# A retention and mixture-of-experts kernel on one core: first loads swapped, two weight blocks ahead of the sorted rows, count sums on GpSimd, totals and head rows one step earlier

## The chip, the cores and the metric

The kernel runs on one core of a Trainium2 chip. The core has a matrix engine (TensorE, PE in the profile; its weight loads are a row of their own, PEld), a vector engine (VectorE, DVE), an activation engine (ScalarE, ACT), a general engine (GpSimd, POOL) and an engine that here mostly issues transfers (SyncE, SP; its rows in the profile are SPq). Each takes its own instructions in order and waits for others by semaphores. Transfers between device memory and on-chip memory (SBUF) run on 16 DMA engines. Matmuls write to PSUM, which has eight banks of 2 KB in each of the 128 partitions. The metric is the device time of one execution in microseconds (us).

## What is computed

Four sequences of 768 tokens with 8 heads of 64 go through retention (attention without softmax, whose state decays by a factor for each head), and the 3072 resulting rows of 512 through a layer of 8 experts. Each row goes to the expert with the largest gate logit alone.

```python
def _attn_ref(q, k, v):                      # B=4, H=8, S=768, D=64
    gamma = 1.0 - 2.0 ** (-5.0 - np.arange(H))
    for t in range(S):
        state = gamma[None, :, None, None] * state + np.einsum('bhd,bhe->bhde', k[:, :, t], v[:, :, t])
        y[:, :, t] = scale * np.einsum('bhd,bhde->bhe', q[:, :, t], state)

def _moe_ref(x, w_gate, w_output_gate, w1, w2):   # x 3072x512, w1 8x512x1024, w2 8x1024x512
    logits = x @ w_gate
    e_idx = np.argmax(logits, axis=1)
    gate_w = softmax(logits)[np.arange(N), e_idx]
    eom = 1.0 / (1.0 + np.exp(-(x @ w_output_gate)))
    for e in range(E):
        mask = e_idx == e
        h = np.maximum(x[mask] @ w1[e], 0.0)
        out[mask] = gate_w[mask, None] * eom[mask, e, None] * (h @ w2[e])
```

## The kernel before

The instructions of each engine stand in the order in which the program is written; no scheduler moves them. So an instruction that waits holds everything that is written behind it for the same engine.

**Start.** SP loads the keys of chunk 0, then the queries (one load serves two chunks of a channel), then those of chunk 1. PE runs matmuls on zeros (`warm_up`) until the keys have come; `kt_block` turns the keys and `qt_block` the queries with PE transposes.

**Chunk loop.** 24 chunks of 128 tokens, one a step, in two channels: even steps belong to channel 0, odd ones to channel 1. A step `n` multiplies the queries with the carried state (`inter`, L348) and with the keys (`scores`, L356, into the banks `s`), masks the scores on DVE (`masked`, L364, `am`), multiplies with the values (`values`, L374, into the banks `y`), scales on DVE (`outputs`, L394, `yt`) and updates the state (`state`, L383, copied to `sd` on ACT). GpSimd scales the values of the next chunk (`prep_v`, L310, `vs`).

Two chunks form a group for the routing, which runs through the following steps. At the end of an odd step PE makes the group's logits (L403, into the bank `misc`), and ACT keeps them (`lt`, L408). In the next even step PE turns them (`turn_logits`, L414), eight small DVE operations choose the expert (`route1`, one-hot `oh`) and ACT takes the exponentials (`exps`). In the odd step after that PE counts the rows ahead of each row (`counts`, L450 to L455), DVE adds the one-hots to the running sums (`acc`, L460) and works out the row's place (`rk` L462, `pos` L465), all in `route2`, ahead of `values` in the program; and at the end of the step, behind the next group's logits, four DVE operations make the gate weight (`gates`, L473 to L477, with scratch in `misc`). PE transposes the finished chunk (`tokens`, L486, into one of two PSUM buffers `px`), ACT scales it by the gate (`rows_out`, L493, `row`), and GpSimd scatters the rows to their expert's region of a sorted table `srt` in device memory (`scatter`, L502).

In step 14 and again in step 18 PE adds up the running sums (`totals`, L517, in `misc`, right after `inter`): the first chooses the early expert, whose number SP loads one step later, the second (with `cj` on DVE, L657) its count so far. From step 17 on weight blocks come in: a block is 128 of an expert's 1024 inner columns, 512 KB in three transfers (`load_weights`, L171 and L175, into four buffers `raw`). ACT rounds it to `whi` (`split_high`, L187, L188), DVE and GpSimd subtract to `wlo` (`split_low`, L195, L196), so that a product is made of three matmuls. After step 20 SP loads the first 256 sorted rows of the early expert (`head_load`, L537); `head_prep` turns them on DVE, half in step 22 and half at the end of step 23, where the row numbers are worked out too (`token_ids`).

**After the loop.** The head (first 256 rows of the early expert, L564 and L582) keeps PE busy in pieces (`run_head`), while the last group is routed and scattered, the experts are ordered by their counts (`order`) and GpSimd clears the row behind each region (`clear`). Then SP loads the sorted rows of pass 0, the other 192 columns of the early expert (`load_x(0)`, L815, `xl`), and seven register loads of `order` (L953). Pass 0 and the seven experts run over 8 blocks each: `mm1` (L873, into `h`), `relu1` (ACT `hh` L882, DVE `hl` L883), `mm2` of the block before (L896, into `a`). Weight blocks are loaded in order, each once its buffer is free; pass 0 starts with blocks 8 and 9, then the next expert's rows are loaded (`load_x(1)`), then block 10 and on. In the last four blocks of a pass `prep_x` turns a quarter of the next expert's rows each (DVE `xt` L836, ACT `xh` L837, DVE `xw` L838); GpSimd sends the finished rows out (`emit`, L203). The last expert's blocks are accumulated row by row (`stage2_last`, L924) and sent by `emit_last`.

Of the kernel before, what the change touches and what calls it, by code (L numbers as in the profile page):

```python
# [33 lines left out]
def retention_moe_kernel(  # L34
# [191 lines left out]
    with ExitStack() as actx:  # L226
# [57 lines left out]
        for b in range(2):  # L284
            nc.vector.memset(sp[b], 0.0)
        load_k(0)
        load_q(0, 0)
# [168 lines left out]

        def route2(grp):
            n = len(grp)
            oh = rt.pop("oh")
            nc.vector.tensor_tensor(out=acc[:, 0:n], in0=acc[:, 0:n], in1=oh, op=ALU.add)  # L460
# [8 lines left out]
        def gates(grp):  # L469
            n = len(grp)  # L470
            ex = rt.pop("ex")
            se, den = small[:, 10 * E:10 * E + 2], small[:, 10 * E + 2:10 * E + 4]
# [71 lines left out]
        def head_prep(g):  # L544
# [7 lines left out]
            if g == 1:  # L552
                hd["idx"] = hpool.tile([P, HEAD // 32], I32, name="idx0")
                tmp = hpool.tile([P, HEAD // 32], I32, name="tmp0")
                token_ids(hd["idx"], t[:, :, P], slot[:, 0:HEAD // 32], cnt0, tmp, False)

        def head_stage1(f):
# [3 lines left out]
            for r, ls in (("xh", (hi, lo)), ("xl", (hi,))):  # L561
                for dc in range(NDC):
# [59 lines left out]
        warm_up(misc, 9)  # L622
        kt_block(0)
        warm_up(misc, 2)
        for r in range(2):
            q_copy(0, 0, r, nc.vector)
        for r in range(2):
            qt_block(0, 0, r, nc.vector if r == 1 else None)
# [10 lines left out]
        for n in range(NCH):  # L639
# [10 lines left out]
            if n in w_at:  # L650
                load_weights(w_at[n])
            inter(n)
            if n == PICK_AT:
                by = rank_key(totals(n), io8)
            if n == EARLY_AT:
                cj = sm.tile([P, E], F32, name="cj", tag="cj")
                nc.vector.scalar_tensor_tensor(out=cj, in0=totals(n), scalar=1.0, in1=first, op0=ALU.mult, op1=ALU.mult,  # L657
                                               accum_out=cnt0)
# [18 lines left out]
            if even and n >= 4:  # L677
                tokens(n - 3)
# [16 lines left out]
            if even and n >= 4:  # L695
                rows_out(n - 3)
            values(n)
            outputs(n)
            state(n)

            for t in turn.get(n, ()) if not soon else ():
                qt_block(*t)
            if not even and n >= 3:
                tokens(n - 3)
            if not even:
# [4 lines left out]
                if grp:  # L710
                    gates(grp)
# [11 lines left out]
            if n - 1 in w_at:  # L723
                split_high(w_at[n - 1])
# [8 lines left out]
            if n == LOAD_AT:  # L733
                head_load()
# [15 lines left out]
        counts(grp, True)  # L750
        route2(grp)
        gates(grp)
# [47 lines left out]
    with ExitStack() as mctx:  # L800
# [149 lines left out]
        arms = {}  # L950
        load_x(0)
        for r in range(1, E):
            rank_e[r] = nc.values_load(order[0:1, r - 1:r], engines=(ET.SP,), min_val=0, max_val=E - 1)  # L953
# [15 lines left out]
        loaded = split = NF  # L969
        for s in range(NS + 1):  # L970
# [168 lines left out]
```

## Time and profile before

| | us |
|---|---|
| median of 3 runs (lowest to highest) | 444.88 (443.98 to 445.35) |
| profiled execution | 442.21 |
| its span in the profile | 440.4 |
| PE busy (share of the span) | 417.7 (95%) |
| VectorE busy | 230.8 (52%) |
| ScalarE busy | 191.2 (43%) |
| GpSimd busy | 255.8 (58%) |
| mean granted TensorE clock | 0.996 |

The profile is of one execution; its own time is 442.21 us, and the span leaves out what lies around the instructions. Busy shares are averages over stages that have different limits. PE's stages are the start (to about 14 us), the chunk loop (to 138), the head (to 164), pass 0 (to 191), the seven other experts (to 428) and the tail. Times in the rows are counted from the start of the span.

### The profile page before, as it was taken

To read this page: it belongs to the slowest core of one execution; us is meant where nothing else is said; L and a number is where in the kernel's file an instruction comes from. 1 tells how busy PE (TensorE), PEld (TensorE's weight loads), DVE (VectorE), ACT (ScalarE), POOL (GpSimd) and SP (SyncE) were. 2 spreads that over 40 slices of the span, in tenths; PEclk is the share of its full clock that TensorE was granted. 3 is DMA by queue.
4 is the path that set the end of the run, shared out by engine and by line. 5 is a ranking of instruction groups with operands and counts; after the bars stand their busy time and mean duration, and the time that the engine had idled before them with its cause. 6 is when DMAs were issued, how large, how long until landed. Compare 5 with 4: busy or idle time off the path is not lost.

```text
span 440.4 us, 10495 instructions
## 1 busy us (share of the span) xinstructions
PE 417.7 (95%) x3600; PEld 382.8 (87%) x3600; DVE 230.8 (52%) x593; ACT 191.2 (43%) x375; POOL 255.8 (58%) x292
## 2 busy tenths in 40 slices
PE   8999899999997999899999999998999999999992
PEld 4778687787786999789999999998999999999881
DVE  3465767666678854672553544454355356354110
ACT  2456455555656423553443443443354354353110
POOL 1555644444549605577237687685776877884712
PEclk9999999999999999999999999999999999999998
DMA  9999989679446529999368459549458848740102
GB/s 200 194 225 267 245 211 230 161 191 245 128 132 208 199 77 229 229 207 235 100 164 205 125 174 227 167 147 215 148 154 186 219 153 190 224 125 10 50 16 71
DMA packets 128381, 75.75 MB, mean 172 GB/s; under 512 B 57748, under 2 KB 116504, under 8 KB 128288
## 3 DMA queue, kind: packets, MB, share of 16 engines
q1 hardware_dynamic: 120896, 59.15, 56.5%
q0 software_dynamic: 5776, 14.76, 9.5%
q8 instruction: 61, 1.00, 1.0%
q10 hardware_dynamic: 1616, 0.57, 0.7%
q14 instruction: 32, 0.26, 0.2%
HBM read 59.71 MB, written 15.30 MB: 170 GB/s over the span
## 4 chain that ended last, share of the span: by engine, by line
PE 78%; DVE 6%; DMA 4%; issue 4%; ACT 3%; POOL 1%; SPq 1%; DVEq 0%; POOLq 0%; ACTq 0%
PE h L873 25%; PE a L896 24%; PE s L356 5%; PE y L374 5%; PE y L348 2%; PE px L486 2%; PE y L564 2%; PE pq L329 2%; DMA qn<-in_q_dram 2%; PE pk L315 2%; PE a L924 2%; PE s L582 2%; PE st L383 2%; PE misc L403 2%; DMA xl<-srt 1%
## 5 line engine op out<-in xcount | busy, mean ns | idle before, releaser
L196 POOL TENSOR_TENSOR wlo<-raw,whi 128x512 fp32r<-128x512 f32 x59 | 78.3, 1328 | 56.0 <-ACT whi L188 46.0
L203 POOL DMA_INDIRECT out_dram<-ot,idi x85 | 86.0, 1012 | 22.5 <-issue 17.7
L873 PE MATMUL h<-xh,whi 128*128 128x192 f32 (+7 forms) x256 | 85.1, 333 | 2.2 <-issue 1.5
L873 PE MATMUL h<-xw,whi 128*128 128x192 f32 (+7 forms) x256 | 85.0, 332 | 0.2 <-DVE xw L838 0.2
L873 PE MATMUL h<-xh,wlo 128*128 128x192 f32 (+7 forms) x256 | 84.7, 331 | 0.0
L883 DVE SCALAR_TENSOR_TENSOR hl<-h,hh 128x192 fp32r<-128x192 f32 (+7 forms) x64 | 35.5, 555 | 88.5 <-ACT hh L882 88.4
L896 PE MATMUL a<-hh,whi 128*128 128x192 f32 (+6 forms) x224 | 74.6, 333 | 1.5 <-ACT hh L882 1.5
L896 PE MATMUL a<-hl,whi 128*128 128x192 f32 (+6 forms) x224 | 74.6, 333 | 0.1
L896 PE MATMUL a<-hh,wlo 128*128 128x192 f32 (+6 forms) x224 | 74.3, 332 | 0.0
L882 ACT ACTIVATE hh<-h 128x192 fp32r<-128x192 f32 (+7 forms) x64 | 31.3, 489 | 77.4 <-PE h L873 77.4
L195 DVE TENSOR_TENSOR wlo<-raw,whi 128x512 fp32r<-128x512 f32 x62 | 42.7, 689 | 31.5 <-ACT whi L187 29.1
L187 ACT CAST whi<-raw 128x512 fp32r<-128x512 f32 x64 | 39.5, 617 | 41.0 <-PE a L896 34.4
L873 PEld LDWEIGHTS h<-xh,whi 128*128 128x128 f32 x256 | 48.2, 188 | 3.5 <-issue 1.8
L873 PEld LDWEIGHTS h<-xw,whi 128*128 128x128 f32 x256 | 48.2, 188 | 1.0 <-DVE xw L838 0.5
L873 PEld LDWEIGHTS h<-xh,wlo 128*128 128x128 f32 x256 | 48.2, 188 | 0.2
L502 POOL DMA_INDIRECT srt<-row,pos x24 | 24.6, 1026 | 36.0 <-ACT qr L321 22.3
L896 PEld LDWEIGHTS a<-hh,whi 128*128 128x128 f32 x224 | 42.2, 188 | 2.2 <-ACT hh L882 1.9
L896 PEld LDWEIGHTS a<-hl,whi 128*128 128x128 f32 x224 | 42.2, 188 | 0.7 <-DVE hl L883 0.4
L896 PEld LDWEIGHTS a<-hh,wlo 128*128 128x128 f32 x224 | 42.2, 189 | 0.3
L310 POOL TENSOR_TENSOR vs<-vn,gv 128x512 f32<-128x512 f32 x24 | 24.9, 1039 | 28.9 <-DMA vn<-in_v_dram 14.6
L188 ACT CAST whi<-raw 128x512 fp32r<-128x512 f32 x64 | 39.5, 616 | 0.4 <-DMA raw<-in_moe_w_dram 0.4
L364 DVE TENSOR_TENSOR am<-s,mask 128x512 f32<-128x512 f32 x48 | 30.9, 686 | 15.8 <-PE s L356 15.4
(170 smaller groups left out, 652.0 us busy)
## 6 DMA issues: line engine op xcount, KB each, us to landing
raw<-in_moe_w_dram SPq DMA_DIRECT2D x128, 128.0 KB, 4.1
raw<-in_moe_w_dram SPq DMA_DIRECT2D x64, 256.0 KB, 3.9
kn<-in_k_dram SPq DMA_DIRECT2D x24, 256.0 KB, 4.9
qn<-in_q_dram SPq DMA_DIRECT2D x12, 512.0 KB, 6.3
vn<-in_v_dram SPq DMA_DIRECT2D x23, 256.0 KB, 5.3
xl<-srt SPq DMA_DIRECT2D x12, 209.6 KB, 6.2
xl<-srt SPq DMA_DIRECT2D x8, 225.8 KB, 7.7
xl<-srt SPq DMA_DIRECT2D x8, 193.5 KB, 5.6
```

What stands on the lines that cost most here:

```text
L187: nc.scalar.copy(hi[:, 0], raw[:, 0])
L188: nc.scalar.copy(perm(hi), r2)
L195: (first or nc.vector).tensor_sub(lo[:, 0], raw[:, 0], hi[:, 0].bitcast(F32))
L196: (second or nc.gpsimd).tensor_sub(perm(lo), r2, perm(hi).bitcast(F32))
L203: st = nc.gpsimd.indirect_dma_start(out=dst, out_offset=bass.IndirectOffsetOnAxis(ap=idx, axis=0), in_=src, in_offset=None, bounds_check=n ...
L310: nc.gpsimd.tensor_mul(vs[i], vn.pop(i), gv[:, c, :].unsqueeze(2).broadcast_to([P, H, D]))
L364: nc.vector.tensor_tensor(out=a.rearrange("p s o t -> p (s o) t"), in0=sp[b].rearrange("p (x t) -> p x t", t=P), in1=mask.unsqueeze(1).bro ...
L502: s_ = nc.gpsimd.indirect_dma_start(out=srt, out_offset=bass.IndirectOffsetOnAxis(ap=rt.pop(("pos", i)), axis=0), in_=row.rearrange("p a x ...
L873: nc.tensor.matmul(ps[:, 0:C], l[:, 0, w], r[:, dc, 0:C], start=(n == 0), stop=(n == 3 * NDC - 1))
L882: nc.scalar.activation(hh, ps[:, 0:C], AF.Relu)
L883: nc.vector.scalar_tensor_tensor(out=hl, in0=ps[:, 0:C], scalar=0.0, in1=hh.bitcast(F32), op0=ALU.max, op1=ALU.subtract)
L896: nc.tensor.matmul(accs[d][:, 0:C], l[:, 1, w], r[:, 0:C], start=(f == 0 and n == 0), stop=(f == NF - 1 and n == 2))
```

## The change

It has these parts.

1. Start: the queries of chunk 0 are loaded ahead of its keys, and copied and turned ahead of them; the copies are spread over DVE and ACT, and two of the matmuls on zeros go.
2. The running sums (`acc`) are added on GpSimd (`add_counts`), for all groups but the last.
3. `gates` moves from the end of the odd step to right behind `route2`; its scratch is a corner of the bank `s` instead of `misc`.
4. `totals` with what reads it moves from step 14 to the end of step 13, and from step 18 to the end of step 17.
5. Some transposes (`tokens`) of the odd steps go ahead of the values, and those of steps 22 and after the loop are moved; `split_high` goes ahead of the values in even steps.
6. `head_load` stands at the start of step 20, `head_prep(0)` at the end of step 21, and the row numbers (`head_ids`) behind the loop. `head_stage1` multiplies the first half of the columns with all three parts, then the second.
7. Behind the head's routing SP loads one register, weight blocks 8 and 9, then pass 0's rows, then the six other registers. In pass 0 the next expert's rows and block 10 therefore come first.
8. Tail: the last block but one is accumulated for two row groups before the last block begins.

```diff
-        load_k(0)
         load_q(0, 0)
+        load_k(0)
...
+        def add_counts(grp, eng):
+            eng.tensor_tensor(out=acc[:, 0:len(grp)], in0=acc[:, 0:len(grp)], in1=rt["oh"], op=ALU.add)
+
         def route2(grp):
             n = len(grp)
             oh = rt.pop("oh")
-            nc.vector.tensor_tensor(out=acc[:, 0:n], in0=acc[:, 0:n], in1=oh, op=ALU.add)
...
-        def gates(grp):
+        def gates(grp, tmp):
+            ex = rt.pop("ex")
             n = len(grp)
-            ex = rt.pop("ex")
-            se, den = small[:, 10 * E:10 * E + 2], small[:, 10 * E + 2:10 * E + 4]
+            se, den = tmp[:, 0:2], tmp[:, 2:4]
...
-            for r, ls in (("xh", (hi, lo)), ("xl", (hi,))):
-                for dc in range(NDC):
+            for r, ls, dcs in [(r, ls, g) for g in ((0, 1), (2, 3)) for r, ls in (("xh", (hi, lo)), ("xl", (hi,)))]:
+                for dc in dcs:
...
+        for r in range(2):
+            q_copy(0, 0, r, nc.vector if r == 0 else nc.scalar)
+        for r in range(2):
+            qt_block(0, 0, r, nc.vector)
         kt_block(0)
-        warm_up(misc, 2)
-        for r in range(2):
-            q_copy(0, 0, r, nc.vector)
-        for r in range(2):
-            qt_block(0, 0, r, nc.vector if r == 1 else None)
...
+            if n == LOAD_AT:
+                head_load()
             inter(n)
-            if n == PICK_AT:
-                by = rank_key(totals(n), io8)
-            if n == EARLY_AT:
-                cj = sm.tile([P, E], F32, name="cj", tag="cj")
...
                 counts(grp)
+                add_counts(grp, nc.gpsimd)
                 route2(grp)
+                gates(grp, sp[0][:, 0:4])
...
+            fill = not even and n > 4 and not turn.get(n, ())
...
+            if fill:
+                tokens(n - 3)
...
-            if n == LOAD_AT + 2:
-                head_prep(0)
-            if even and n >= 4:
+            if even and 4 <= n < NCH - 2:
                 rows_out(n - 3)
+            if even and n - 1 in w_at:
+                split_high(w_at[n - 1])
             values(n)
             outputs(n)
             state(n)
+            if n == NCH - 2:
+                tokens(n - 3)
+                rows_out(n - 3)
...
+            if n == PICK_AT - 1:
+                by = rank_key(totals(n), io8)
+            if n == EARLY_AT - 1:
+                cj = sm.tile([P, E], F32, name="cj", tag="cj")
...
-            if not even and n >= 3:
+            if not even and n >= 3 and not fill:
                 tokens(n - 3)
...
-                if grp:
-                    gates(grp)
...
-            if n == LOAD_AT:
-                head_load()
+            if n == LOAD_AT + 1:
+                head_prep(0)
...
         scatter(NCH - 4)
+        tokens(NCH - 3)
         turn_logits(grp)
-        tokens(NCH - 3)
+        split_high(NF - 4)
         rows_out(NCH - 3)
         route1(grp)
         exps(grp)
+        head_ids()
...
+        load_rank(1)
+        for s in (NF, NF + 1):
+            load_weights(s)
         load_x(0)
-        for r in range(1, E):
-            rank_e[r] = nc.values_load(order[0:1, r - 1:r], engines=(ET.SP,), min_val=0, max_val=E - 1)
+        for r in range(2, E):
+            load_rank(r)
...
-        loaded = split = NF
+        loaded, split = NF + 2, NF
...
-                for tb in range(NTB):
-                    for z in (NS - 2, NS - 1):
-                        stage2_last(z, tb)
+                for tb in range(2):
+                    stage2_last(NS - 2, tb)
+                for tb in range(NTB):
+                    if tb >= 2:
+                        stage2_last(NS - 2, tb)
+                    stage2_last(NS - 1, tb)
                     emit_last(tb)
```

What stands in a row on VectorE in an odd step of the loop, from the masks to the next step's masks, before (names are out<-in; `misc` and `s_126` are PSUM banks):

```order
L364 TENSOR_TENSOR am_448<-s_127,mask 128x512
L460 TENSOR_TENSOR acc<-acc,oh 128x16
L462 TENSOR_TENSOR misc<-misc,oh 128x16
L465 TENSOR_REDUCE pos<-misc 128x2
L394 TENSOR_TENSOR yt<-y_129,gq 128x2x128
L394 TENSOR_TENSOR yt<-y_130,gq 128x2x128
L473 TENSOR_REDUCE misc<-ex 128x2
L474 TENSOR_SCALAR misc<-misc 128x2
L475 SCALAR_TENSOR_TENSOR misc<-ex,misc 128x2
L477 RECIPROCAL gate<-misc 128x2
```

The same step on VectorE after the change:

```order
L364 TENSOR_TENSOR am_446<-s_127,mask 128x512
L464 TENSOR_TENSOR misc<-misc,oh 128x16
L467 TENSOR_REDUCE pos<-misc 128x2
L475 TENSOR_REDUCE s_126<-ex 128x2
L476 TENSOR_SCALAR s_126<-s_126 128x2
L477 SCALAR_TENSOR_TENSOR s_126<-ex,s_126 128x2
L479 RECIPROCAL gate<-s_126 128x2
L394 TENSOR_TENSOR yt<-y_129,gq 128x2x128
L394 TENSOR_TENSOR yt<-y_130,gq 128x2x128
```

The sum is gone from VectorE, and the four gate operations stand ahead of the two `yt`.

On PE the totals of step 13 and 14 (`ones_b` is a matrix of ones; after `state`, ahead of the transposes `px` and the logits, where the two lines of the difference stand with +):

```order
 L383 MATMUL st<-vs,kn 64x64 x8
-L486 MATMUL px<-ident,yt 128x128 x4
+L519 LDWEIGHTS ones_b
+L519 MATMUL misc<-acc,ones_b 128x8
+L519 LDWEIGHTS ones_b
+L519 MATMUL misc<-acc,ones_b 128x8
+L488 MATMUL px<-ident,yt 128x128 x4
 L403 MATMUL misc<-yt,wg 32x256 x4
 L348 MATMUL y_129<-qt,sd 64x128
```

They stood between the next step's state product (L348) and its scores (L356) before.

On SP, from pass 0's rows on, before (the two numbers behind a region are rows of 32 and their count):

```order
L815 DMA xl<-srt 32x6x129
L953 TENSOR_LOAD order
L953 ISA x2
L171 ISA
L171 DMA raw<-in_moe_w_dram 64x4x128
L175 ISA
L175 DMA raw<-in_moe_w_dram 128x512
L815 ISA
L815 DMA xl<-srt 32x14x129
```

The same place on SP after the change:

```order
L967 TENSOR_LOAD order
L967 ISA x2
L171 ISA
L171 DMA raw<-in_moe_w_dram 64x4x128
L175 ISA
L175 DMA raw<-in_moe_w_dram 128x512
L829 ISA
L829 DMA xl<-srt 32x6x129
L829 ISA
L829 DMA xl<-srt 32x14x129
```

Only one row of each repetition is shown. The two weight blocks stood between the two loads of sorted rows and now stand ahead of both.

## Rows read from the trace of the kernel before

**Rows 1.** Busy time of the engines: busy us (share of the span) xinstructions

```profile
PE 417.7 (95%) x3600; PEld 382.8 (87%) x3600; DVE 230.8 (52%) x593; ACT 191.2 (43%) x375; POOL 255.8 (58%) x292
```

**Rows 2.** What PE waited for, 10 to 140 us: us in total, times, longest

```profile
PE misc L414 <- DVE gate L477: 1.8, 2, 1.5
...
PE misc L517 <- DVE gate L477: 1.4, 2, 0.7
...
PE pq L329 <- ACT qr L321: 0.6, 1, 0.6
```

**Rows 3.** What PE waited for, 140 to 441 us

```profile
PE a L896 <- ACT hh L882: 1.5, 2, 0.8
```

**Rows 4.** Busy time by stage: length, engines (xinstructions), PE clock, DMA share, GB/s

```profile
138.00:164.00 26.00, 24.72 (x209) 24.51 (x210) 18.38 (x72) 11.45 (x26) 11.16 (x14) 1.00 0.48 157
164.00:191.00 27.00, 24.50 (x198) 23.05 (x197) 16.32 (x36) 12.54 (x27) 15.60 (x14) 1.00 0.93 224
```

**Rows 5.** The chain that ended last: start us, us, what

```profile
3.04 8.80 DMA qn<-in_q_dram
...
168.14 6.22 DMA xl<-srt
174.49 4.56 DMA raw<-in_moe_w_dram
```

**Rows 6.** Timeline of step 7: start us, us, engine line [idle before <-releaser]

```profile
49.52 2.83 DVE L460 TENSOR_TENSOR acc<-acc,oh 128x16 bf16<-128x16 bf16 x1
...
50.88 0.66 PE L486 MATMUL px<-ident,yt 128*128 128x128 f32 x4
...
51.28 1.03 POOL L310 TENSOR_TENSOR vs<-vn,gv 128x512 f32<-128x512 f32 x1
...
53.03 0.96 PE L403 MATMUL misc<-yt,wg 128*32 128x256 f32 x8 [1.49 <-DVE yt L394]
```

**Rows 7.** Timeline of step 19, VectorE and GpSimd

```profile
115.37 0.17 DVE L462 TENSOR_TENSOR misc<-misc,oh 128x16 f32<-128x16 f32 x1
115.38 1.26 POOL L196 TENSOR_TENSOR wlo<-raw,whi 128x512 fp32r<-128x512 f32 x1
```

**Rows 8.** Timeline of step 17, VectorE and PE

```profile
104.27 0.86 DVE L394 TENSOR_TENSOR yt<-y,gq 128x256 f32<-128x256 f32 x2
...
105.64 0.64 PE L403 MATMUL misc<-yt,wg 128*32 128x256 f32 x8
...
106.75 0.18 DVE L473 TENSOR_REDUCE misc<-ex 128x2 f32<-128x16 f32 x1 [1.62 <-ACT lt L408]
...
107.37 0.17 DVE L477 RECIPROCAL gate<-misc 128x2 f32<-128x2 f32 x1
```

**Rows 9.** Timeline of SP's queue in pass 0

```profile
162.15 1.46 SPq L171 DMA_DIRECT2D raw<-in_moe_w_dram  x2
...
167.05 1.94 SPq L815 DMA_DIRECT2D xl<-srt  x4
```

**Rows 10.** Timeline of pass 0, ScalarE, VectorE and PE

```profile
170.04 0.33 ACT L882 ACTIVATE hh<-h 128x192 fp32r<-128x192 f32 x1 [0.31 <-PE h L873]
...
172.72 0.33 ACT L882 ACTIVATE hh<-h 128x192 fp32r<-128x192 f32 x1 [0.31 <-PE h L873]
...
178.40 0.32 ACT L882 ACTIVATE hh<-h 128x192 fp32r<-128x192 f32 x1
...
180.22 0.64 DVE L836 STREAM_TRANSPOSE xt<-xl 128x448 f32<-128x448 f32 x1
...
190.61 0.47 PE L873 MATMUL h<-xw,whi 128*128 128x432 f32 x1 [0.19 <-DVE xw L838]
```

**Rows 11.** What SP's queue waited for, 140 to 200 us

```profile
SPq L815 <- DMA srt<-zrow,endr: 9.1, 1, 9.1
```

**Rows 12.** The first sorted rows `xl`, 150 to 170 us: uses (start us) and landing

```profile
L221 DVE TENSOR_TENSOR tmp<-tmp,xl x1: 170/170/170, 160.0 to 160.0; 128x6 int32<-128x6 int32 x1
...
DMA to landing us min/median/max: 2.1/2.1/2.1
```

More of the change, by code (lines that the diff above doesn't have):

```diff
@@ L285, in retention_moe_kernel @@
             nc.vector.memset(sp[b], 0.0)
+        load_q(0, 0)
         load_k(0)
-        load_q(0, 0)
         nc.scalar.activation(warm, warm, AF.Exp)
@@ L551, in head_prep, with head_ids @@
             nc.gpsimd.tensor_sub(hd["xl"][:, 2 * g:2 * g + 2], tp, hd["xh"][:, 2 * g:2 * g + 2].bitcast(F32))
[L552 to L555, printed above, removed]
+        def head_ids():
+            t = hd["t"]
+            hd["idx"] = hpool.tile([P, HEAD // 32], I32, name="idx0")
+            tmp = hpool.tile([P, HEAD // 32], I32, name="tmp0")
+            token_ids(hd["idx"], t[:, :, P], slot[:, 0:HEAD // 32], cnt0, tmp, False)
         def head_stage1(f):
@@ L651, in retention_moe_kernel @@
                 load_weights(w_at[n])
+            if n == LOAD_AT:
+                head_load()
             inter(n)
-            if n == PICK_AT:
-                by = rank_key(totals(n), io8)
-            if n == EARLY_AT:
-                cj = sm.tile([P, E], F32, name="cj", tag="cj")
-                nc.vector.scalar_tensor_tensor(out=cj, in0=totals(n), scalar=1.0, in1=first, op0=ALU.mult, op1=ALU.mult,
-                                               accum_out=cnt0)
             scores(n)
@@ L686, in retention_moe_kernel @@
                 counts(grp)
+                add_counts(grp, nc.gpsimd)
                 route2(grp)
+                gates(grp, sp[0][:, 0:4])
             soon = not even and len(turn.get(n, ())) == 1
+            fill = not even and n > 4 and not turn.get(n, ())
             if soon:
                 qt_block(*turn[n][0])
+            if fill:
+                tokens(n - 3)
             if even and n - 2 in w_at and n < 22:
                 split_low(w_at[n - 2])
-            if n == LOAD_AT + 2:
-                head_prep(0)
-            if even and n >= 4:
+            if even and 4 <= n < NCH - 2:
                 rows_out(n - 3)
+            if even and n - 1 in w_at:
+                split_high(w_at[n - 1])
             values(n)
@@ L699, in retention_moe_kernel @@
             state(n)
+            if n == NCH - 2:
+                tokens(n - 3)
+                rows_out(n - 3)
             for t in turn.get(n, ()) if not soon else ():
                 qt_block(*t)
-            if not even and n >= 3:
+            if n == PICK_AT - 1:
+                by = rank_key(totals(n), io8)
+            if n == EARLY_AT - 1:
+                cj = sm.tile([P, E], F32, name="cj", tag="cj")
+                nc.vector.scalar_tensor_tensor(out=cj, in0=totals(n), scalar=1.0, in1=first, op0=ALU.mult, op1=ALU.mult,
+                                               accum_out=cnt0)
+            if not even and n >= 3 and not fill:
                 tokens(n - 3)
@@ L722, in retention_moe_kernel @@
                 exps(grp)
-            if n - 1 in w_at:
+            if not even and n - 1 in w_at and n < NCH - 1:
                 split_high(w_at[n - 1])
@@ L750, in retention_moe_kernel @@
         counts(grp, True)
+        add_counts(grp, nc.vector)
         route2(grp)
-        gates(grp)
+        gates(grp, small[:, 10 * E:10 * E + 4])
         run_head(6)
@@ L950, in retention_moe_kernel, with load_rank @@
         arms = {}
+        def load_rank(r):
+            rank_e[r] = nc.values_load(order[0:1, r - 1:r], engines=(ET.SP,), min_val=0, max_val=E - 1)
+        load_rank(1)
+        for s in (NF, NF + 1):
+            load_weights(s)
         load_x(0)
-        for r in range(1, E):
-            rank_e[r] = nc.values_load(order[0:1, r - 1:r], engines=(ET.SP,), min_val=0, max_val=E - 1)
+        for r in range(2, E):
+            load_rank(r)
         PASS += [(rank_e[r] * REG, CAPS[r - 1]) for r in range(1, E)]
```

## The prediction

> **What bounds the kernel now.** I read the busy shares first: TensorE (PE) has work for 417.7 us of the span of 440.4 [rows 1], so some 22 us at most can be won without taking matmuls away, and this change takes almost none away. Next the waits of PE, in two stretches: in the chunk loop it stands still for single reasons of 0.6 to 1.5 us each [rows 2], after the loop for ScalarE's relu in the first pass of the sorted rows [rows 3]. The busy time by stage shows where the second kind lies: between 164 and 191 us PE works 24.50 of 27.00 us while the DMA engines are at 0.93, and in the stage before, 138 to 164, they are at 0.48 [rows 4]. Last the chain that ended last: it holds the landing of chunk 1's queries at the start, and much later the load of the second expert's rows followed by one weight block [rows 5]. So two sorts of edit can pay: one that takes a stall of PE out of the loop, and one that moves DMA work from 164 to 191 into the emptier stage ahead. The profiled execution took 442.21 us, 2.67 under the median of 444.88; the sum below is a difference against the profiled one and is taken off the median.
>
> **Queries ahead of keys: 0.** Chunk 1 is released by its queries, issued at 3.04 and landed 8.80 us later [rows 5]. The change only swaps the first two loads ahead of them, so the bytes in front stay the same. Chunk 0 may finish earlier and then waits for chunk 1. Bounds: 0.6 either way, what a late query copy cost PE in another step [rows 2].
>
> **Count sums on GpSimd: +1.8.** In step 7 the sum L460 on VectorE (DVE) took 2.83 us, 49.52 to 52.35, and ended when GpSimd's `vs`, begun at 51.28, ended after its 1.03. Behind it stood rank, position and the two `yt`, and PE, done with the transposes at 50.88 + 0.66 = 51.54, started the logits at 53.03 and took 0.96 for them [rows 6]; undisturbed logits take 0.64 [rows 8]. Without the sum, six small operations at 0.2 each (rank, position, four gates) let `yt` start about 50.8, and the logits run 51.54 to 52.18 and not to 53.99: 1.81. The lower end is 0, if the hold passes to the next DVE operation. Against that speaks step 19, where the rank L462 took 0.17 beside a GpSimd subtraction of 1.26 [rows 7]; I take the upper end. On GpSimd the small sum stands behind the scatter, and only the counts two steps later read it.
> The Trainium skill (GPSIMD Engine Reference, Key points) says that GpSimd shares its SBUF interfaces with VectorE and that VectorE instructions with two SBUF inputs contend. L460 has two such inputs, the rank reads one of its two from PSUM: by that rule the hold would not pass on and the time would be the 438.1 below; if any DVE operation can be held, it is the 439.9 of the fourth rival. Step 19 agrees with the rule, in one instance.
>
> **Totals one step up: +1.4.** The two totals waited 1.4 us in all, 0.7 the longer, for the gates that stood ahead of them in the same PSUM bank [rows 2]. Now they stand at the end of the odd step ahead of the transposes, and the gates write another bank. Their own matmuls stay. Bounds 0.8 to 1.45: the operation that reads the totals is one more of 0.2 on DVE, twice, and may push what comes next.
>
> **Gates in line: -0.15.** In step 17 the four gate operations ran from 106.75 to 107.37 + 0.17, 0.79 us, after the logits; DVE had idled 1.62 us before them, waiting for ScalarE to read the bank [rows 8]. Now they stand ahead of `yt`, in place of the sum. `yt` then starts some 0.6 us later than its 104.27, so it ends at about 105.75 and not at 105.13; the logits, at 105.64, need its second half only 0.32 later [rows 8]. So a usual step pays 0. In the last two odd steps the transposes move away from in front of the logits, there is less cover, and I charge 0.15. Worst end: 1.0 for those two and a few others; best 0.
>
> **Weight split ahead of the values: +0.4.** In step 19 PE waited 0.6 us for a query copy on ScalarE [rows 2] that was queued behind a weight cast. In steps 18, 20 and 22 the cast now goes earlier; bounds 0 to 0.6.
>
> **Loop end: +0.15.** The last turned logits waited 1.5 us for the gates [rows 2]. That wait goes, and transposes fill part of the place. But the head's second matmuls then wait for DVE, which still has the eight routing operations, the row numbers and a weight subtraction ahead of the half that they need, so most of the 1.5 comes back there. Bounds -0.5 to +0.6.
>
> **Two weight blocks ahead of the sorted rows: +3.4.** This is the large term. Before, two blocks held SP's queue from 162.15 until the second expert's rows went out at 167.05 [rows 9]. Those rows took 6.22 to land, and one block after them held the chain 4.56 more [rows 5]. ScalarE's relus stand at 170.04, 172.72 (2.68 apart, PE's pace) and then 178.40 [rows 10]. The two blocks now go out before the first sorted rows, while SP stood still for 9.1 us [rows 11] and the DMA engines were half idle [rows 4]. So the second expert's rows go out at 162.15 or a little before, 4.9 earlier, and the block behind them too. The late relu then falls at 172.72 + 2.68 = 175.40, 3.0 earlier. Behind it DVE prepares four pieces of the next expert's rows from 180.22 on; the last of these released PE at 190.61 [rows 10]. That train, 10.39 long, keeps its length, and starts 3.4 earlier: 3.0 from the relu, and 0.4 of the 1.82 between relu and first piece, where DVE reads row numbers. Bounds: 2.5 if a later block still lands late; 3.9 if half of the 1.82 goes.
>
> **What that does to the first sorted rows: -0.2.** Their load waited 9.1 us for the clearing of row ends [rows 11], landed in 2.1, and DVE used it at 160.0, at once [rows 12]. One MB of weights now moves while the clears do. The stage has room: half of its 26 us at 224 GB/s, the rate of the stage after [rows 4], is 2.9 MB. So I charge 0.2; the upper end is the first rival.
>
> **Tail: 0.** The two last weight blocks are accumulated in another order, with the same matmuls and the same three sends after them, which hide what PE gains. Bounds 0 to 0.8, the price of a wait for a relu in the first pass [rows 3].
>
> **Sum.** 1.8 + 1.4 - 0.15 + 0.4 + 0.15 + 3.4 - 0.2 = 6.8, so 442.21 becomes 435.4 profiled, and the median 444.88 becomes **438.1**.
>
> **Rivals.**
> First: the weight blocks make the first sorted rows late. For it: SP issues both, and the blocks now stand ahead; the second expert's rows took 6.22 in a full stage [rows 5], the first ones 2.1 [rows 12], 4.1 less. Against it: the half-idle stage. If all 4.1 fell on PE, 6.8 + 0.2 - 4.1 = 2.9 are left: 442.0.
> The Trainium skill (DMA: Bandwidth & Descriptors, Queues, rings and completion order) states that each DMA engine takes the descriptors of one ring in order, so that what SP issued first is fetched first; this speaks for the rival, and no row of before shows the two transfers in that order.
> Second: pass 0 keeps its length because the DMA engines stay at 0.93 there [rows 4] and later blocks arrive as late as before. Then 3.4 falls away: 441.5.
> Third, **slower**: the gates are not covered. They are 0.79 us in each of 11 odd steps; if DVE's work ahead of `yt` set each step's end, that is 8.7, against gains of 6.95 without this term: 1.75 slower, 446.6. It decides from 6.95 / 11 = 0.63 us per step. Against it: the cover in step 17 [rows 8], and the place that the sum leaves.
> Fourth: the hold of step 7 passes to another DVE operation, or returns in another step: 439.9.
> Fifth: nothing of it moves the end, since each stall is replaced by the next one: 444.9.
>
> **How the numbers follow.** Chances: forecast, with its small terms, 0.60; late first rows 0.08; pass 0 as long 0.12; hold moved 0.11; no change 0.05; slower 0.04. All upper ends together win 9.75 (0.6 + 1.8 + 1.45 + 0 + 0.6 + 0.6 + 3.9 + 0 + 0.8): 435.1. Low ends of the forecast (0.8 for the totals, 2.5 for the pass, 0 for the split) give 440.2; the second rival, which the range must also hold, 441.5. So the range is 435.1 to 441.6. About 0.3% (1.3 us) is what a measurement of this kernel can tell from no change. Faster 0.90, same 0.06, slower 0.04.
>
> **What would show it.** Right: no sum on DVE in the loop, and the logits of step 7 right behind the transposes; no wait for a gate in PE's list; the second expert's rows issued about 5 us earlier against the head's end; the relus of pass 0 evenly 2.7 apart; the last prepared piece no longer 18 us behind the relu at 172.72 but under 15. Wrong: DVE's first use of the sorted rows over 1 us later against the head's end, `yt` ending well after the transposes in most odd steps, or weight waits in pass 0 as before.

## The result, and the profile after

The changed kernel takes 437.66 us (437.14 to 438.06, 4 runs) against 444.43 (443.12 to 445.35, 4 runs) beside it: ratio 0.9849, 95% interval 0.982 to 0.9878, that is 6.8 us, between 5.4 and 8.0. The forecast was 438.1, 6.8 less than 444.88. The profiled execution took 437.51 us with a span of 435.7; the profiled one of before took 442.21, which is below every one of before's four runs here. So the two profiles differ by only 4.7, and a good part of this text is about the other 2.

The busy times after answer [rows 1]: PE is as busy as before, in a shorter span.

```profile
PE 417.4 (96%) x3598; PEld 381.7 (88%) x3598; DVE 224.9 (52%) x582; ACT 189.7 (44%) x375; POOL 257.2 (59%) x303
```

What PE waited for, 10 to 140 us, against [rows 2] (us in total, times, longest). No wait for a gate is left, neither the 1.8 nor the 1.4, and the 1.49 for `yt` in step 7 [rows 6] is gone too. New are two smaller waits for `yt`, both in step 23 (0.7 ahead of the logits, 0.5 ahead of the product with the state), and one for the keys at the start.

```profile
PE pq L329 <- ACT qr L321: 0.9, 2, 0.7
PE pk L315 <- DMA kn<-in_k_dram: 0.8, 1, 0.8
PE s L356 <- ACT qt L331: 0.7, 1, 0.7
PE misc L403 <- DVE yt L394: 0.7, 1, 0.7
PE y L348 <- DVE yt L394: 0.5, 1, 0.5
```

And from 138 us on, against [rows 3]: the waits for the relu in pass 0 are gone; one for the head's relu (L573) has come.

```profile
PE a L938 <- issue: 0.6, 1, 0.6
PE s L586 <- ACT h L573: 0.4, 1, 0.4
```

Step 7, against [rows 6]: the sum is on GpSimd (L458, 0.21), `yt` runs while PE transposes, and the logits start right behind the transposes and take 0.64. All timelines here read: start us, us, engine line.

```profile
51.01 0.21 POOL L458 TENSOR_TENSOR acc<-acc,oh 128x16 bf16<-128x16 bf16 x1
...
51.32 0.73 DVE L394 TENSOR_TENSOR yt<-y,gq 128x256 f32<-128x256 f32 x2
...
51.70 0.66 PE L488 MATMUL px<-ident,yt 128*128 128x128 f32 x4
...
52.29 0.64 PE L403 MATMUL misc<-yt,wg 128*32 128x256 f32 x8
```

Busy time by stage, against [rows 4] (length, PE, PEld, DVE, ACT, POOL with counts, clock, DMA share, GB/s): DMA work has moved from pass 0 (0.93 to 0.79) into the head (0.48 to 0.67), and PE has 26.47 of 27 us where it had 24.50.

```profile
138.00:164.00 26.00, 25.04 (x204) 23.88 (x203) 17.48 (x66) 9.93 (x24) 9.16 (x12) 1.00 0.67 188
164.00:191.00 27.00, 26.47 (x215) 25.67 (x215) 18.86 (x45) 13.82 (x30) 18.32 (x16) 1.00 0.79 202
```

Pass 0, against [rows 10]: the fourth and fifth relu are 2.7 apart (5.7 before), the first prepared piece comes at 176.15, and the last one releases PE at 186.53, 14.8 us behind the relu at 171.72 (17.9 before).

```profile
171.72 0.33 ACT L896 ACTIVATE hh<-h 128x192 fp32r<-128x192 f32 x1 [0.31 <-PE h L887]
...
174.40 0.33 ACT L896 ACTIVATE hh<-h 128x192 fp32r<-128x192 f32 x1 [0.31 <-issue]
...
176.15 0.64 DVE L850 STREAM_TRANSPOSE xt<-xl 128x448 f32<-128x448 f32 x1
...
186.53 0.47 PE L887 MATMUL h<-xw,whi 128*128 128x432 f32 x1 [0.19 <-issue]
```

The queue of SP, against [rows 9]: both blocks go out at 147.54 and 151.58, and behind them the two loads of sorted rows, shown as one line from 154.83 to 162.36; the second of them begins at 160.45.

```profile
147.54 1.44 SPq L171 DMA_DIRECT2D raw<-in_moe_w_dram  x2
...
151.58 1.42 SPq L171 DMA_DIRECT2D raw<-in_moe_w_dram  x2
...
154.83 7.53 SPq L829 DMA_DIRECT2D xl<-srt  x8
```

To see what each part did I follow the same events through two timelines and note by how much the changed kernel leads. The second column is another profile of the same changed kernel (e9 below), on another chip. A stretch is what the lead grows by from one event to the next; each is a difference of start times (logits: their end) in the timelines.

| stretch, up to | forecast | first profile | second (e9) |
|---|---|---|---|
| chunk 1's scores | 0 | -0.87 | -0.50 |
| logits of step 7 | +1.8 | +1.93 | +1.56 |
| logits of step 19 (totals, weight split) | +1.8 | +1.79 | +2.70 |
| logits of step 23 | -0.15 | -1.09 | -1.10 |
| head's first relu (loop end) | +0.15 | +0.62 | +0.63 |
| head's seventh relu | 0 | -0.34 | -0.04 |
| pass 0's first relu | -0.2 | -1.04 | -1.37 |
| next expert's first relu (pass 0) | +3.4 | +3.08 | +3.38 |
| last relu | 0 | -0.20 | +0.46 |
| last send | 0 | 0 | 0 |
| end of the span | 0 | +0.82 | +0.68 |
| sum | 6.8 | 4.70 | 6.4 |

### The profile page after: what moved, and what is told of

Read it like the earlier page. It is cut to its first block, busy times and chain, and to the rows that moved or that the text cites. A ratio compares the mean times of both kernels' runs of the same rounds, so it can differ in the third digit from the quotient of the medians.

```text
span 435.7 us, 10494 instructions
## 1 busy us (share of the span) xinstructions
PE 417.4 (96%) x3598; PEld 381.7 (88%) x3598; DVE 224.9 (52%) x582; ACT 189.7 (44%) x375; POOL 257.2 (59%) x303
## 4 chain that ended last, share of the span: by engine, by line
PE 73%; issue 8%; POOL 5%; DMA 4%; DVE 3%; ACT 3%; SPq 1%; POOLq 0%; DVEq 0%; ACTq 0%
PE h L887 26%; PE a L910 24%; PE s L356 5%; PE y L374 4%; PE y L348 3%; PE px L488 2%; DMA qn<-in_q_dram 2%; PE pq L329 2%; POOL out_dram L203 2%; PE pk L315 2%; PE st L383 2%; PE misc L403 2%; POOL wlo L196 1%; DMA srt<-zrow,endr 1%; PE misc L414 1%
## 5 line engine op out<-in xcount | busy, mean ns | idle before, releaser
L195 DVE TENSOR_TENSOR wlo<-raw,whi 128x512 fp32r<-128x512 f32 x62 | 43.8, 706 | 29.4 <-PE a L910 8.7
```

The lines of the kernel that those rows point to most:

```text
L195: (first or nc.vector).tensor_sub(lo[:, 0], raw[:, 0], hi[:, 0].bitcast(F32))
```

## The experiments

Ratios are to runs of the kernel before on the same chip, with their 95% interval. Each group of four ran on a chip of its own (e1 to e4, e5 to e8, e9 to e12), and before's median was 443.13, 449.95 and 442.97 us on them, with runs from 439.1 to 453.3. The ratios resolve some 0.3 to 0.5%; what is smaller is read from the timelines. "Lead" is against the one profile of before.

**e1: the sums on GpSimd alone.**

```diff
-            nc.vector.tensor_tensor(out=acc[:, 0:n], in0=acc[:, 0:n], in1=oh, op=ALU.add)
+            (nc.gpsimd if grp[0] < NCH - 2 else nc.vector).tensor_tensor(out=acc[:, 0:n], in0=acc[:, 0:n], in1=oh, op=ALU.add)
```

> The kernel before with one part of the change alone: the count sums on GpSimd for all groups but the last. Theory 1 (the hold of L460 in step 7 is the whole gain of this part): 1.9 us faster than before, about 442.5 against 444.4, and in its profile the logits of step 7 start right behind the transposes. Theory 2 (the hold falls on other steps too, in executions that were not profiled; the change's medians differ by 6.8 us where the two profiles differ by only 4.7): 2.5 to 4 us faster, and the runs scatter less than before's 443.1 to 445.4. Theory 3 (the hold passes on to another VectorE operation): 0 to 0.5 faster, and a rank, position or yt of over 1 us in the profile.

Measured: 440.12 us (12 runs), ratio 0.9948 (0.992 to 0.9975), 2.3 us faster, 1.1 to 3.5. The lead at the logits goes from -0.65 in step 5 to +1.22 in step 7: 1.87, as in the changed kernel. No other VectorE operation took the hold over. Between the first two theories the interval does not decide, and the 12 runs scatter over 4.6 us (437.96 to 442.54), the 23 of before over 6.9.

**e2: the changed kernel with the sums back on VectorE.**

```diff
-                add_counts(grp, nc.gpsimd)
+                add_counts(grp, nc.vector)
```

> The changed kernel with the count sums back on VectorE, all other parts kept. Theory 1: one long sum holds yt in some step, 1.5 to 1.9 us slower than the changed kernel's 437.7, about 439.4. Theory 2 (the hold is a matter of where GpSimd's work happens to fall, and falls on nothing in the new order): within 0.5 of 437.7, with all sums at 0.16 to 0.3 us in the profile. Theory 3 (several holds): over 2.5 slower.

Measured: 437.84 us (6 runs), ratio 0.989 (0.9855 to 0.9925). Four sums are long, 0.55, 0.75, 1.51 and 1.25 us, in steps 3, 7, 19 and 21. Two of them with what GpSimd did beside:

```profile
112.64 1.51 DVE L458 TENSOR_TENSOR acc<-acc,oh 128x16 bf16<-128x16 bf16 x1
112.84 1.27 POOL L196 TENSOR_TENSOR wlo<-raw,whi 128x512 fp32r<-128x512 f32 x1
...
114.07 0.17 DVE L464 TENSOR_TENSOR misc<-misc,oh 128x16 f32<-128x16 f32 x1
```

```profile
123.95 1.25 DVE L458 TENSOR_TENSOR acc<-acc,oh 128x16 bf16<-128x16 bf16 x1
...
124.14 1.03 POOL L310 TENSOR_TENSOR vs<-vn,gv 128x512 f32<-128x512 f32 x1
...
125.13 0.17 DVE L464 TENSOR_TENSOR misc<-misc,oh 128x16 f32<-128x16 f32 x1
```

In both the sum ends with GpSimd's operation (114.11 and 125.17; the sums 114.15 and 125.20), and PE waits for `yt` 2.8 us in all from step 19 on (0.7 of it in step 23, as in the changed kernel):

```profile
PE misc L403 <- DVE yt L394: 2.8, 3, 1.2
```

The head's first relu is 1.93 later than in the changed kernel (142.30 against 140.37). On the same chip e4, which differs from e2 by the start as well, took 435.06, 2.8 less: that fits the third theory, several holds, better than the first. So the hold hangs on where GpSimd's work falls. In the four profiles with the sums on VectorE (before, e2, e3, e8) each of the fourteen sums of 0.3 us and more ends within 0.05 us of a GpSimd tensor operation; beside a scatter alone a sum took 0.16 (135.81 in before).

**e3: the new order on SP alone** (the kernel before with one register, blocks 8 and 9, then the rows, as in the change).

> The kernel before with the new order on SP behind the loop alone: one register, two weight blocks, then the first sorted rows. From the two profiles pass 0 got 3.1 us shorter and the head 1.0 longer, because the first sorted rows came late and ScalarE's last relu of the head stood behind their copies. Theory: both come with this part, so 2.1 us faster than before, about 442.3, with pass 0 (first matmul to the last piece's) near 23.0 and not 26.1. Rival: the shorter pass needs the earlier head of the changed kernel, and this part alone gives under 0.7.

Measured: 441.06 us (12 runs), ratio 0.9947 (0.9922 to 0.9973), 2.3 us faster, 1.2 to 3.5. Both effects come with this part alone: from the head's seventh relu to pass 0's first it loses 1.21, and pass 0 is 3.38 shorter, 2.17 in sum. So the earlier head is not needed.

**e4 and e10: the changed kernel with the start of before**, on two chips.

```diff
-        load_q(0, 0)
         load_k(0)
+        load_q(0, 0)
...
-        for r in range(2):
-            q_copy(0, 0, r, nc.vector if r == 0 else nc.scalar)
-        for r in range(2):
-            qt_block(0, 0, r, nc.vector)
         kt_block(0)
+        warm_up(misc, 2)
+        for r in range(2):
+            q_copy(0, 0, r, nc.vector)
+        for r in range(2):
+            qt_block(0, 0, r, nc.vector if r == 1 else None)
```

> The changed kernel with the start of before: keys of chunk 0 loaded ahead of its queries, turned first, and the two matmuls on zeros kept. In the changed kernel's profile the scores of chunk 1 began 0.87 us later than before (15.32 against 14.45), since its queries landed at 12.8 and not 11.9. Theory: that loss belongs to the swap, and this kernel is 0.9 faster than the changed one, about 436.8, with chunk 1's scores at 14.5. Rival: the landing scatters from execution to execution and the two are within 0.3.

> The kernel of e4 again (changed kernel with the start of before), now on the same chip as the changed kernel. Theory: the swap of the first two loads costs 0.6 to 0.9 us, so this is 0.15% to 0.2% faster than the changed kernel, and the scores of chunk 1 start that much earlier in its profile. Rival: under 0.2 us in the scores of chunk 1; then what e4 showed was scatter of the first transfers.

Measured: e4 435.06 us, ratio 0.9824 (0.9792 to 0.9857); e10 436.18, ratio 0.9846 (0.9812 to 0.9881), beside the unaltered changed kernel (e9) at 435.0, ratio 0.9814. The same kernel is thus on either side of the changed one, and beside e9 it was the slower one by 1.2 us, within the intervals. Chunk 1's scores start at 14.68 and 14.59, and at 14.95 in e9; at the logits of step 3 e10 and e9 are only 0.15 apart (30.98 and 31.13). About half of the 0.87 of the first profile was scatter: with before's start the scores began between 14.45 and 15.10 in ten profiles (mean 14.8; and once, in e8, at 18.01), with the new one at 15.32, 15.38 and 14.95 (mean 15.22). The other half goes with the swap: SP issues chunk 1's queries at 3.42 to 3.52 in these three, and at 2.87 to 3.04 in all eleven with before's start. My theory of 0.6 to 0.9 falls, and so does the rival of under 0.2 (0.36 here); the 0.4 that the profiles show is less than the timed runs can tell.

**e5: the gates of steps 21 and 23 behind `yt` again**, on e4.

```diff
                 route2(grp)
-                gates(grp, sp[0][:, 0:4])
+                if n < 21:
+                    gates(grp, sp[0][:, 0:4])
...
             outputs(n)
+            if not even and n >= 21:
+                gates(grp, sp[0][:, 0:4])
```

> The kernel of e4 (changed kernel, start of before) with the gates of steps 21 and 23 alone put behind yt again. In e4's profile the lead over before shrinks by 1.1 us between the logits of step 21 and those of step 23, and the changed kernel's by the same 1.1. Theory (the gates ahead of yt are no longer covered where the transposes have moved away): the lead at the logits of step 23 grows by about 1.0 and 0.5 or more of it reaches the end; some 0.2% faster than e4's 0.9824 of before. Rival (the values themselves come later there, from GpSimd or the masks): the logits of step 23 move by under 0.3.

Measured: 439.67 us, ratio 0.9776 (0.9727 to 0.9825). The lead still falls by 1.34 from step 21 to step 23 (e4: 1.10). So the gates are not what costs there.

**e6: both loads of sorted rows ahead of the blocks**, on e4. **e7: one block ahead, the other behind the registers**, on e4.

```diff
         load_rank(1)
-        for s in (NF, NF + 1):
-            load_weights(s)
+        PASS.append((rank_e[1] * REG, CAPS[0]))
         load_x(0)
+        load_x(1)
+        for s in (NF, NF + 1):
+            load_weights(s)
```

```diff
         load_rank(1)
-        for s in (NF, NF + 1):
-            load_weights(s)
+        load_weights(NF)
         load_x(0)
         for r in range(2, E):
             load_rank(r)
+        load_weights(NF + 1)
```

> The kernel of e4 with another order on SP behind the loop: one register, both loads of sorted rows (pass 0's and the next expert's), then the two weight blocks, then the other registers. Theory (the two blocks made the first rows late, which cost 1.2 to 1.3 us at the head's end in e3 and e4; the shorter pass 0 comes from the next expert's rows and block 10 being early, not from blocks 8 and 9): the head's last relu keeps its lead (about -3.7 against before, not -2.3), pass 0 stays at its 3.4 less, so 1.2 faster than e4. Rival (blocks 8 and 9 then come too late for pass 0): the third relu of pass 0 waits, and pass 0 is 1 to 3 us longer than in e4.

> The kernel of e4 with only the first of the two weight blocks ahead of the first sorted rows, the second behind the registers. Theory: half of the lateness, so the head's last relu gains some 0.6 on e4's, and pass 0 keeps its length since the next expert's rows still go out 3 us before the old time; 0.6 faster than e4. Rival: the lateness comes from the clears sharing the DMA engines with any block, and stays at 1.2.

Measured: e6 441.47 us, ratio 0.9827 (0.979 to 0.9865); e7 441.61, ratio 0.9821 (0.9773 to 0.9869). In e6 the rows are in time: DVE uses them 1.2 us behind the head's seventh relu (158.0 and 156.83), as before (160.0 and 158.94, 1.1), while in the changed kernel it was 2.2 (159.14 and 156.90) and in e3 2.4.

```profile
L221 DVE TENSOR_TENSOR tmp<-tmp,xl x1: 171/171/171, 158.0 to 158.0; 128x6 int32<-128x6 int32 x1
```

The head's end then loses nothing (the lead at pass 0's first relu is that of the head's seventh, 2.11), but pass 0 wins only 2.3 and not 3.4: what is saved at one end is given back at the other, with block 10 issued at 167.37 and not at 162.63. In e7 the last relu of the head loses nothing and pass 0 wins 3.35. But one of ScalarE's gaps (e9, below) stood in e7's head, which took 21.63 us from the logits of step 23 to the seventh relu, against 20.59 in e4, so that the rows had 1.0 us more; without the gap, in e12, it did not hold.

**e8: two more matmuls on zeros at the start of the kernel before.**

```diff
-        warm_up(misc, 3)
+        warm_up(misc, 5)
```

> The kernel before with two more matmuls on zeros at the start, so that everything behind them stands two instructions later in PE's program. In the three profiles with before's program on PE there is a gap of 1.3 to 1.8 us ahead of block 33's first matmul, in which PE waits for nothing that the profile shows; in the three with the changed program it is 0.2 to 0.3. Theory (the gap hangs on where the instructions lie): it moves or goes, and the lead at block 34 grows by about 1.2. Rival (it hangs on what the other engines and the DMA do there): it stays at 1.3 to 1.8.

Measured: 451.3 us in one execution, on the chip where before takes 449.95. The gap is there, 1.83 us, but two matmuls earlier in the program. Ahead of it stand four matmuls of the block, where before (and e1 and e3) six stood:

```profile
308.23 0.45 PE L873 MATMUL h<-xw,whi 128*128 128x392 f32 x1 [1.83 <-issue]
```

and in the kernel before:

```profile
303.47 0.45 PE L873 MATMUL h<-xh,whi 128*128 128x392 f32 x1 [1.51 <-issue]
```

So it hangs on the place in PE's instruction stream: two more ahead, and it strikes two earlier. It did not go, as the theory had left open, and no lead was won. The changed programs agree: without the two extra matmuls at the start (the changed kernel, e2, e9) the gap stands behind the twelfth and last matmul of a block, with them (e4, e6, e7, e10 to e12) ahead of that matmul, and in e5 one matmul earlier still.

**e9: the changed kernel again.**

> The changed kernel once more, unaltered, beside the next three on one chip. If the gain of the change is what its first comparison gave (0.9849 of before), it is 0.980 to 0.990 here. In its first profile two gaps of ScalarE with no cause in the profile stood at the head's fourth relu and at the last pass's fifth (3.7 and 7.4 us long); if they belong to the chip's state and not to the program, they are gone or of another length here.

Measured: 435.0 us (6 runs), ratio 0.9814 (0.9781 to 0.9847). Neither of ScalarE's two long gaps of the first profile is there; its table column is the second one above. In the first profile they read:

```profile
150.08 0.39 ACT L573 ACTIVATE h<-y 128x256 fp32r<-128x256 f32 x1 [3.66 <-remote]
```

```profile
414.00 0.48 ACT L896 ACTIVATE hh<-h 128x368 fp32r<-128x368 f32 x1 [7.41 <-PE h L887]
```

The second cost 1.0 us of lead (4.90 at the relu before it, 3.88 at the last), the first 0.3. They stand in e5, e6, e7 and e8 too, at the same relus, where the second costs 4.0 to 6.4 us and PE waits behind it for 2.1 to 3.6; not in e1 to e4 or e9 to e12. So they go with the chip and with the place in the program; what they are is not shown.

**e11: the transposes of step 23 between values and logits again**, on e4. **e12: e11 with one block ahead.**

```diff
-            fill = not even and n > 4 and not turn.get(n, ())
+            fill = not even and 4 < n < NCH - 1 and not turn.get(n, ())
```

> The kernel of e4 with the transposes of step 23 back between its values and its logits. In e5 the logits of step 23 still waited 0.69 us for yt although the gates had left the way, and yt itself 0.63 for the values. Theory (the 1.1 us lost in step 23 come from the transposes that no longer stand there): the logits of step 23 lose under 0.2 against step 21, so they are about 1.0 earlier than e10's, and 0.5 or more of it reaches the head's last relu. Rival: the head's first matmuls then wait for VectorE or GpSimd, and at the head's last relu under 0.2 is left.

> The kernel of e11 with only one weight block ahead of the first sorted rows, as in e7. Theory: the parts add up; the head's last relu comes without the delay of 1.0 to 1.4 us, pass 0 keeps its length, and the kernel is 0.3% to 0.5% faster than e10, that is about 0.978 of before. Rival: the earlier head makes the first rows late again, and it equals e11.

Measured: e11 434.81 us, ratio 0.982 (0.9785 to 0.9854); e12 435.52, ratio 0.9837 (0.9804 to 0.987). The wait of the logits for `yt` in step 23 is gone from PE's list, and yet the lead falls by 1.11 from step 21 to step 23, as in e10: the transposes take the time that was the wait. The theory falls. What is left in the timeline of e11 stands in step 22:

```profile
126.82 1.16 PE L374 MATMUL y<-am,vs 128*64 128x128 f32 x16
...
127.92 0.66 PE L488 MATMUL px<-ident,yt 128*128 128x128 f32 x4
128.61 0.76 DVE L394 TENSOR_TENSOR yt<-y,gq 128x256 f32<-128x256 f32 x2 [1.34 <-PE px L488]
129.09 0.99 PE L348 MATMUL y<-qt,sd 64*64 64x128 f32 x16 [0.52 <-DVE yt L394]
```

and in the kernel before:

```profile
130.23 0.60 PE L486 MATMUL px<-ident,yt 128*128 128x128 f32 x4
...
131.20 1.09 PE L374 MATMUL y<-am,vs 128*64 128x128 f32 x16
...
132.39 1.09 PE L348 MATMUL y<-qt,sd 64*64 64x128 f32 x16
```

The transposes of chunk 19 stand behind the values of step 22 in the change. Before, they stood ahead of them, where PE would else have waited for the masks. `yt` of step 22 waits for them, since it writes the buffer of two groups ago that they read, and the state product of step 23 waits for `yt`. From values to state product it is 2.27 us now and 1.19 before (126.82 to 129.09, 131.20 to 132.39), while from scores to values only 0.30 is won (2.03 against 2.33); with 0.32 in step 23, where the logits wait for the second `yt` (0.96 long, 0.64 before), that is the loss. That this is the cause was read, not tried.

In e12 the last relu of the head still loses 1.11, and pass 0 wins 2.87: from the head's seventh relu to the next expert's first nearly what e11 wins (1.86 and 1.97). No kernel here is shown to beat the changed one; e4, e9, e11 and e12 lie within each other's intervals.

## Why the prediction was right, step by step

The time was right, and the largest step of the loop was too. But the sum of 6.8 held in the medians partly because errors of both signs met.

**Right in kind and size.** The sums on GpSimd: 1.8 forecast, 1.87 between steps 5 and 7 in the first profile, e1 and e9. Totals and weight split: 1.8 forecast, 1.79 between steps 7 and 19 in the first profile, 2.70 in e9. No run takes these two parts alone. In the first profile and in e9 the lead grows by 0.92 from step 13 to 15, and by 1.47 and 1.64 from step 17 to 19, which is where the totals' two waits and the query copy's stood; in e1, without these parts, it falls by 0.09 and 0.15 there. The Trainium skill (GPSIMD Engine Reference, Key points) says that GpSimd contends with VectorE instructions that have two SBUF inputs. e2 agrees: the sum was held four times, the rank, position and gates stood at 0.17. The fourth rival fell with it: no other operation took over the hold. The swap at the start: 0 forecast, within 0.6; the profiles show a loss of some 0.4, since chunk 1's queries go out some 0.5 later, which the forecast, counting bytes alone, left out.

**Right in kind, wrong in size: the weight blocks.** Pass 0 got 3.08 shorter (3.4 forecast), by the mechanism that was named: relus at an even pace, the train of four pieces with an unchanged length, 186.53 - 176.15 = 10.38. But the first sorted rows, charged at 0.2, cost 1.04 to 1.37: this is the mis-sized term, and e3, e4 and e6 tie it to this part. It is also one of the prediction's own signs of being wrong: against the head's seventh relu DVE first used the rows 1.15 us later, in e9 1.5. It was not the way of the first rival: their landing took 2.2 us in e9, as before (2.1), and not 6. What came later is the release, since SP still waits for the clears, which now share the DMA engines with a block: from the start of the third clear to the issue of the rows it is 3.47 us before and 3.56 in e6, but 4.72 in the changed kernel and 5.04 in e9. And ScalarE, in order, held the head's last relu behind the copies of the late rows. I had counted the room in the stage, not when the clears need it. The Trainium skill (DMA: Bandwidth & Descriptors, Queues, rings and completion order) says that each DMA engine takes the descriptors of one ring in order. By that rule the rows' own transfer would have been the slow one; no run here shows that.
Besides, the long pass 0 of the profiled before may not be its usual one: its fourth and fifth relu lie 5.68 apart there, but 4.29 in e1 and 4.85 in e8, which have the same order on SP. From the head's seventh relu to the next expert's first those two are 1.39 and 0.82 shorter than the profile I had, so by these profiles, of several chips, the gain of this part is nearer 1.3 (a mean of 2.04 in the eight kernels with both blocks ahead, less 0.74 in the three with before's order) than the 3.2 forecast. e3's timed 2.3 (1.2 to 3.5) allows both 1.3 and 3.2.

**Wrong: the last two odd steps.** Forecast -0.15, with -1.0 as the worst end; measured -1.09 and -1.10. The step that failed is the cause as well: I had put it on the gates, and e5 shows that it isn't them. The move of step 22's transposes stood in no term of the sum; by the rows of e11 and before they stood where PE else waits for the masks, and now they hold `yt`'s buffer. That this is the cause is read from the rows and not tried.

**Wrong on the good side: the loop end.** 0.62 and 0.63, not 0.15, just past the upper end of 0.6.

**Not in the sum at all.** A gap of PE of 1.51 us in the second half of the program, with no cause in the profile's waits, is 0.20 there in the changed kernel, 0.3 in e2, e4, e6, e10, e11 and e12, 0.5 in e5, 0.86 in e7, twice 0.5 in e9, and 1.26 to 1.83 in the four profiles with before's program on PE. e8 shows that it is tied to the place in the stream. The traces' transfers show more: in all fourteen profiles one transfer of the queue that the page lists as `q8 instruction` (61 packets, 1.00 MB in the kernel before) lands 1.28 to 1.56 us before PE goes on, however long the gap is (in before it runs from 300.80 to 301.91, and PE goes on at 303.47). So the gap goes with a load of instructions; that PE waits for just this one is inferred from the times. The Trainium skill (Runtime: NRT & Kernel Launch, Instruction fetch mechanics) says that an engine's instructions are refilled in blocks, and that a taken branch to one not at hand stalls. The two-matmul shift agrees with a block's edge; no run shows whether a branch has a part in it. Why the gap is shorter in the changed kernel stays open. Against it stand ScalarE's gaps in the first profile, which cost 1.3.

**The base.** The profiled before (442.21) was 2.2 below its median here, the profiled changed kernel (437.51) 0.15. I took a difference against the one and off the other. With e9's profile, free of ScalarE's gaps, the difference is 6.4; the remaining 0.4 is within the spread of both (on e9's chip the medians differ by 8.0). So 6.8 against 6.8 is in part luck: the sum over-counted pass 0 and the rows by 1.2 (3.2 against 2.04 and 2.01) and the last odd steps by 0.9, and left out 0.5 at the loop's end, 0.7 to 0.8 behind the last send and the shorter gap. The stretch behind the last send is no gain of the change: it is 7.8 us in the profiled before, 7.0 and 7.1 in the changed kernel, and 7.0 in e1, which has before's tail. A slip in the prediction's sums: its low ends give 440.0 (444.88 - 4.9), not 440.2; the range does not hang on it.

## What to carry to other kernels

A small two-input operation on VectorE that now and then takes ten times its length is worth moving, even to a slower engine, if nobody waits for its result soon: the hold hangs on what GpSimd does beside it, so that it can turn up in another step after the next edit (e2). Work that is moved off a wait must be asked what it covered and whose buffer it reads; here the lead fell by 1 us where transposes were moved. And one profile of before is one draw: where a stage waits for DMA, read its length in a second execution before a gain of 3 us is put on it.

## What the runs showed of the hardware

- The 128x16 sum of two SBUF operands took 0.16 us alone and up to 2.83 beside GpSimd operations; in the three cases shown (2.83, 1.51, 1.25) it ended within 0.05 us of one; beside a scatter alone it took 0.16 (135.81 and 143.50 in before); on GpSimd it took 0.21 to 0.23. In step 7 of before it was held over several operations in a row; what held it from 49.60, when the masks ended, to 50.14, when the first tensor operation of GpSimd beside it began, is not shown (a scatter ran then).
- A gap in PE's stream of 1.26 to 1.76 us stayed at its place over three profiles (before, e1, e3), and stood exactly two matmuls earlier, with 1.83, when two were put ahead (e8); a transfer of instructions landed 1.28 to 1.56 us before its end in all fourteen profiles.
- One chip (e5 to e8) showed gaps that cost 4.0 to 6.4 us at one place in the last pass; in the other profiles that place cost 1.0 (the first of the changed kernel) or nothing, with the same program in e9.
